# Scores of both chunks of a pair as one TensorE group, two last output transfers on ScalarE's queue, and a new order of all steps, in a gated linear attention followed by an MLP

## The chip, the cores and the metric

The kernel runs on one core of a Trainium2 chip. The metric is the time of one execution in device microseconds (us). Five engines run side by side, each in its own program order: TensorE (PE, with weight loads shown apart as PEld), VectorE (DVE), ScalarE (ACT), GpSimd (POOL) and SyncE (SP), which here only issues transfers. They meet through semaphores.

## The reference

Inputs q, k, v and a gate logit, each 4 batches x 8 heads x 768 tokens x 48 dimensions in float32; weights w_in 384x2048 and w_out 2048x384.

```python
f = 1 / (1 + exp(-f_logit))
for t in range(768):
    state = f[:, :, t, :, None] * state + k[:, :, t] (outer) v[:, :, t]
    y[:, :, t] = q[:, :, t] @ state
x = y as 3072 tokens x 384            # all heads side by side
h = x @ w_in
out = max(0.01 * h, h) @ w_out        # 3072 x 384, float32
```

## The kernel before, in words

The sequence is cut into chunks of 128 tokens. Two neighbouring chunks of one batch form a pair of 256 tokens; there are twelve pairs, and pair m belongs to batch m % 4. Pairs 0 to 3 are the starts of the four sequences. Every step works on a pair, with w = 0 or 1 for its chunk. A step is a small function with buffer numbers as arguments, and the kernel's last part, from line 451 on, is a list of 766 calls written out one under the other: each engine runs its own share of that list in that order. Nothing is scheduled at run time; an engine waits only for the semaphores of the data and buffers that its next step needs.

The steps of one pair, in the order in which they depend on each other:

- `load('K' | 'Q' | 'V' | 'F', m, s)` (line 255): SP issues the 384 KB of one input of pair m into one of three slots s. A slot is written again only when its readers are done.
- `gate_exp`, `gate_ln` (ACT, lines 259 and 262), `gate_sum` (265), `gate_pe` (TensorE, 268 and 270, a sum over earlier tokens by a triangular matrix), `gate_base` (DVE, 275), `gate_next` (279), then `decay_end`, `decay_em` and `decay_a` (ACT, 282, 285, 288): the products of gates, as exponentials of sums of logarithms.
- `scale` (294): K and Q times their decays, into one of three buffers KH.
- `turn_pe` with `turn_out` (310, 313), or `turn_dma` (305, a transposing transfer on SP's queue): KH turned into KT.
- `score(w, t, bk0, bk1)` (324): eight matmuls of 64 rows x 128 columns with 128 moving columns. Two heads lie above one another, so that the even heads use the lower 64 rows of the array and write one PSUM bank, and the odd heads use the upper 64 rows and write another.
- `mask` (DVE, 333): a bank of scores times a triangular mask, into WM.
- `mix` (TensorE, 342 and 345): WM times the values (`v_cast`, `v_spread` at 302 prepare them), plus Q times the state that the chunk begins with.
- `state_pe` (TensorE, 354, also on 64 rows), `state_dve` (361), `state_pool` (364), `put_state` (POOL, 236): the new state.
- `y_out`, then `x_pe` with `x_out` (381) or `x_dma` (387): the pair's y, turned, in XT.
- `up(g, bk, t)` (392), eight per pair: six matmuls of 256 columns into a PSUM bank; `up_act` (ACT, 408) applies the leaky ReLU.
- `down(w, h, n, bk, t)` (420): the sum over the 2048 inner dimensions, in n parts, four matmuls of 384 columns per part where n is 4, eight where n is 2. `put` copies the bank to SBUF, and `out_pair` (436) sends it. The very last chunk is made in two halves of 192 columns: `down_cols` (425), `put_cols`, `out_cols` (447).

PSUM has eight banks, and a step names the one it uses. `move` (127 on ACT, 129 on DVE and POOL) is the copy behind most steps that empty a bank, and its first argument chooses the engine. The first two pairs go by steps of their own, whose names begin with `f_`. The weights come in by POOL's queue: `load_w_in` twice (246), `load_w_out` four times (249), after `touch` has seen the gate input of pair 1 land. `idle_pe(n, bk)` (133) issues n matmuls on a buffer of zeros.

Of the kernel before, what the change touches and what calls it, by code (L numbers as in the profile page):

```python
# [15 lines left out]
def kernel(  # L16
# [10 lines left out]
    nc = tc.nc  # L27
# [429 lines left out]
    f_cast(V, 0, 1, 0, 1)  # L457
    f_ln(0, 1, 0)
    load('F', 1, 1)
    f_cast(A, 0, 0, 0, 1)  # L460
    f_gate(None, 0, (0, 0 + 1))
    f_cast(G, 0, 0, 1, 2)
# [3 lines left out]
    f_cast(G, 0, 1, 1, 2)  # L466
    idle_pe(2, 7)
    f_cast(V, 1, 0, 0, 1)
    f_turn(0, None, 2, 3)
    f_decay2(0, 'a', 0)  # L470
    f_cast(G, 1, 1, 0, 1)
    f_mul2(0, 0, 2, 0)
    idle_pe(2, 7)
    load('V', 1, 1)
    f_turn(1, None, 1, 4)
    v_cast(G, 0, 0)
    f_back(1, 0, 5)
    f_mul2(0, 1, 4, 0)
    load('Q', 1, 1)
    f_back(0, 0, 2)  # L480
    f_back_out(A, 1, 5)
    v_turn(0, 6, 6 + 1)
    touch('F', 1)
    f_back_out(A, 0, 2)
    load_w_in(0)
    load('K', 2, 2)
    score(1, 0, 0, 0 + 1)
    v_out2(A, 6, 0)
    score(0, 0, 4, 4 + 1)
    load_w_in(1)  # L490
    mask_two(0, 0)
    f_exp(1)
    load('V', 2, 2)
    load_w_out(0)
    f_state_pe(0, 0, 2)
    f_state_pe(1, 0, 6)
    idle_pe(7, 7)
    f_state_dve(0, 2)
    load_w_out(1)
    f_ln(1, 0, 0)  # L500
    load_w_out(2)
    mask_two(4, 2)
    f_ln(1, 1, 0)
    gate_exp(2)
    put_state(0, 0)
    f_gate(None, 0, (0, 0 + 1))
    load('F', 3, 0)
    load_w_out(3)
    state_dve(0, 6)
    f_decay2(1, 'e', 0)  # L510
    mix(0, 0, None, [2, 2 + 1], 0, 7)
    mix(1, 0, (0, 0), [0, 0 + 1], 0, 2)
    v_cast(G, 1, 1)
    y_out(V, 0, 7, 0)
    y_out(A, 1, 2, 0)
    f_mul2(1, 0, 3, 1)
    f_state_pool(0)
    f_decay2(1, 'a', 0)
    v_turn(1, 4, 4 + 1)
    f_cast(G, 1, 1, 1, 2)  # L520
    x_pe(0, 6)
    v_out2(V, 4, 1)
    f_cast(G, 1, 0, 1, 2)
    f_back(1, 1, 7)
    x_out(A, 6, 0)
    f_back(0, 1, 2)
    put_state(0, 1)
    f_turn(1, None, 2, 3)
    f_back_out(A, 3, 7)
    f_back_out(V, 2, 2)  # L530
    f_mul2(1, 1, 3, 1)
    f_state_pe(2, 1, 0)
    gate_ln(2)
    f_state_pe(3, 1, 1)
    up(0, 6, 0)
    gate_sum(G, 2, 0)
    up(1, 7, 0)
    f_state_dve(1, 0)
    up_act(0, 6, 0)
# [12 lines left out]
    mask_two(2, 6)
    f_state_pool(1)
    up(4, 5, 0)
    put_state(1, 1)
    up(5, 6, 0)
    up_act(4, 5, 0)
    gate_base(2, 4)
    mix(0, 1, None, [6, 6 + 1], 1, 0)
    up(6, 1, 0)  # L560
    decay_end(4, 0)
    gate_next(V, 2)
    y_out(A, 0, 0, 1)
    y_out(V, 1, 7, 1)
    up(7, 2, 0)
    decay_a(2, 0)
    down(1, 0, 4, 3, 0)
    up_act(6, 1, 0)
    x_pe(1, 7)
    up_act(7, 2, 0)  # L570
    down(0, 0, 4, 5, 0)
    x_out(V, 7, 1)
    decay_em(2, 0)
    load('F', 4, 1)
    down(0, 1, 4, 5, 0)
    up_act(5, 6, 0)
    up(0, 4, 1)
    up(1, 2, 1)
    up_act(0, 4, 1)
    up(2, 0, 1)  # L580
    up_act(1, 2, 1)
    down(0, 2, 4, 5, 0)
    up_act(2, 0, 1)
    scale(V, 0, 2, 0, 1)
    down(1, 0, 4, 4, 1)
    load('Q', 2, 2)
    down(0, 0, 4, 2, 1)
    v_cast(G, 2, 2)
    down(0, 3, 4, 5, 0)
    load('F', 5, 2)  # L590
    turn_pe(0, 1, 1)
    put(A, 0, 5, 0)
    v_spread(2, 2)
    state_pe(1, 2, 0, 7)
    gate_exp(0)
    down(1, 1, 4, 3, 0)
    load('K', 3, 0)
    gate_ln(0)
    down(1, 2, 4, 3, 0)
    state_first(2, 0, 0)  # L600
    down(1, 3, 4, 3, 0)
    load('Q', 3, 0)
    gate_exp(1)
    gate_sum(G, 0, 1)
    turn_out(V, 0, 1, 2)
    up(3, 6, 1)
    gate_ln(1)
    put(V, 1, 3, 0)
    put_state(2, 0)
    load('Q', 4, 1)  # L610
    up(4, 5, 1)
    up_act(3, 6, 1)
    scale(V, 1, 2, 0, 1)
    gate_pe(1, 3)
    up(5, 0, 1)
    up_act(4, 5, 1)
    out_pair(nc.sync, 0, 1, 0)
    down(0, 1, 4, 2, 1)
    gate_sum(G, 1, 0)
    state_dve(2, 7)  # L620
    gate_exp(2)
    load('V', 3, 0)
    turn_pe(1, 1, 1)
    gate_base(0, 3)
    up_act(5, 0, 1)
    load('V', 4, 1)
    up(6, 5, 1)
    state_pool(2, 1, 0)
    turn_out(V, 1, 1, 2)
    decay_end(3, 1)  # L630
    down(0, 2, 4, 2, 1)
    gate_ln(2)
    put_state(2, 1)
    load('V', 5, 2)
    gate_next(V, 0)
    score(1, 2, 3, 6)
    up_act(6, 5, 1)
    score(0, 2, 7, 0)
    gate_sum(G, 2, 1)
    mask(6, 8)  # L640
    up(7, 1, 1)
    decay_em(0, 1)
    down(1, 1, 4, 4, 1)
    mask(7, 9)
    up_act(7, 1, 1)
    scale(G, 0, 0, 1, 0)
    out_pair(nc.sync, 0, 0, 0)
    down(1, 2, 4, 4, 1)
    mask(0, 10)
    decay_a(0, 1)  # L650
    load('Q', 5, 2)
    down(0, 3, 4, 2, 1)
    mask(3, 11)
    load('F', 6, 0)
    mix(0, 2, None, [9, 10], 2, 5)
    put(A, 0, 2, 1)
    mix(1, 2, (2, 0), [11, 8], 2, 6)
    y_out(V, 0, 5, 2)
    scale(G, 1, 0, 1, 0)
    turn_pe(0, 0, 7)  # L660
    y_out(A, 1, 6, 2)
    down(1, 3, 4, 4, 1)
    load('K', 4, 1)
    turn_out(A, 0, 7, 0)
    x_pe(2, 5)
    gate_pe(1, 1)
    x_out(V, 5, 2)
    gate_pe(0, 0)
    put(A, 1, 4, 1)
    v_cast(G, 1, 0)  # L670
    turn_pe(1, 0, 3)
    gate_base(1, 0)
    load('Q', 6, 0)
    up(0, 2, 2)
    turn_out(A, 1, 3, 0)
    v_cast(G, 0, 1)
    gate_base(2, 1)
    up(1, 6, 2)
    v_spread(0, 0)
    load('V', 6, 1)  # L680
    decay_end(1, 2)
    decay_end(0, 3)
    state_pe(0, 1, 7, 3)
    up_act(0, 2, 2)
    score(0, 0, 5, 4)
    score(1, 0, 1, 0)
    up_act(1, 6, 2)
    up(2, 2, 2)
    load('V', 7, 0)
    gate_next(G, 1)  # L690
    mask(4, 2)
    gate_exp(0)
    up(3, 6, 2)
    state_first(3, 7, 1)
    up_act(2, 2, 2)
    down(1, 0, 4, 4, 2)
    load('K', 5, 2)
    v_cast(G, 2, 2)
    mask(1, 3)
    gate_ln(0)  # L700
    down(0, 0, 4, 7, 2)
    put_state(3, 0)
    mask(0, 0)
    load('V', 8, 2)
    up(4, 2, 2)
    up_act(3, 6, 2)
    gate_sum(V, 0, 1)
    up(5, 1, 2)
    decay_em(1, 0)
    v_spread(1, 1)  # L710
    load('K', 6, 0)
    down(0, 1, 4, 7, 2)
    up_act(5, 1, 2)
    up(6, 6, 2)
    up_act(4, 2, 2)
    out_pair(nc.sync, 1, 0, 1)
    gate_pe(1, 0)
    decay_a(1, 0)
    scale(G, 0, 1, 0, 2)
    mask(5, 1)  # L720
    mix(1, 0, (3, 0), [3, 0], 1, 1)
    out_pair(nc.sync, 1, 1, 1)
    down(0, 2, 4, 7, 2)
    gate_base(0, 0)
    up_act(6, 6, 2)
    load('F', 7, 1)
    mix(0, 0, None, [1, 2], 1, 2)
    up(7, 5, 2)
    decay_end(0, 4)
    y_out(A, 0, 2, 0)  # L730
    v_spread(2, 2)
    down(1, 1, 4, 4, 2)
    load('K', 7, 1)
    y_out(A, 1, 1, 0)
    up_act(7, 5, 2)
    down(1, 2, 4, 4, 2)
    x_pe(0, 6)
    gate_next(G, 0)
    state_dve(3, 3)
    down(1, 3, 4, 4, 2)  # L740
    x_out(A, 6, 3)
    down(0, 3, 4, 7, 2)
    gate_next(V, 2)
    decay_em(0, 1)
    up(0, 5, 3)
    scale(G, 1, 1, 0, 2)
    put(V, 0, 7, 2)
    decay_em(2, 0)
    up(1, 0, 3)
    put(V, 1, 4, 2)  # L750
    turn_pe(0, 2, 1)
    out_pair(nc.sync, 2, 1, 2)
    decay_a(2, 1)
    state_pe(2, 0, 4, 2)
    out_pair(nc.sync, 2, 0, 2)
    turn_out(V, 0, 1, 1)
    scale(G, 0, 0, 1, 1)
    decay_a(0, 0)
    up(2, 3, 3)
    load('F', 8, 2)  # L760
    state_dve(0, 4)
    turn_pe(1, 2, 1)
    load('Q', 7, 1)
    up_act(0, 5, 4)
    up(3, 6, 3)
    load('F', 9, 0)
    turn_out(V, 1, 1, 1)
    up_act(2, 3, 4)
    up(4, 7, 3)
    scale(G, 1, 0, 0, 1)  # L770
    up_act(3, 6, 4)
    score(1, 1, 3, 1)
    up_act(4, 7, 4)
    load('K', 8, 0)
    score(0, 1, 4, 5)
    mask(1, 4)
    up(5, 6, 3)
    up_act(1, 0, 4)
    mask(5, 5)
    up(6, 7, 3)  # L780
    gate_exp(2)
    state_pool(0, 0, 3)
    turn_dma(0, 1, 2)
    mask(4, 6)
    down(1, 0, 2, 1, 4)
    v_cast(G, 2, 1)
    up_act(5, 6, 4)
    mask(3, 7)
    up_act(6, 7, 4)
    put_state(0, 0)  # L790
    turn_dma(1, 1, 2)
    mix(0, 1, (0, 1), [6, 5], 0, 0)
    gate_ln(2)
    v_spread(1, 1)
    up(7, 3, 3)
    load('Q', 8, 0)
    gate_exp(0)
    down(0, 0, 2, 5, 4)
    up_act(7, 3, 4)
    v_cast(G, 1, 0)  # L800
    y_out(V, 0, 0, 1)
    mix(1, 1, (0, 0), [7, 4], 0, 4)
    load('V', 9, 2)
    gate_ln(0)
# [440 lines left out]
```

## Time and profile before

| what | value |
|---|---|
| median of the three runs (lowest, highest) | 179.95 us (179.74, 181.64) |
| the profiled execution's own time | 179.52 us |
| its span on the core | 177.8 us |
| granted TensorE clock, mean | 0.988 |
| TensorE busy | 169.2 us (95%) |
| ScalarE, VectorE, GpSimd busy | 112.9, 107.7, 73.3 us |
| HBM read, written | 25.17, 4.72 MB |

The profiled execution took 179.52 us, of which the span, from the first to the last instruction on the core, is 177.8; the 1.7 us between lie around it. In the profile, a line of a view names an engine, the line of the kernel, and what it writes and reads ("ps" is PSUM). The chain of waits goes back from the last instruction, at each step to what released it; a number behind an x counts instructions. In tables by stretch of time, busy times are given for each engine, with the granted clock of TensorE as a share of full speed.

### The profile page before, as it was taken

How to read it: one execution, taken by the hardware profiler on the slowest of the kernel's cores; microseconds unless marked ns; L12 is line 12 of the kernel's file. 1: busy time of each engine (PE TensorE's matmuls, PEld its weight loads, DVE VectorE, ACT ScalarE, POOL GpSimd, SP SyncE). 2: the span in 40 equal slices, each digit the busy share in tenths (PEclk: the TensorE clock that was granted, in tenths of full speed). 3: DMA queues.
4: the chain of work that ended last, by engine and by line, in shares of the span. 5: the costliest groups of instructions: out<-in, count | busy, mean ns of one | idle time of the engine just before them, and what ended most of it. 6: DMA issues, size and time to landing. Idle time of an engine off the chain costs nothing.

```text
span 177.8 us, 4579 instructions
## 1 busy us (share of the span) xinstructions
PE 169.2 (95%) x1843; PEld 135.0 (76%) x1843; DVE 107.7 (61%) x214; ACT 112.9 (63%) x194; POOL 73.3 (41%) x121
## 2 busy tenths in 40 slices
PE   6977999999999999999999999999999999999991
PEld 4555888677878787688697887787787796877980
DVE  5289693298599969699879592586792830100120
ACT  2978657589779696967284998396273163555700
POOL 7489420177945784595846670204055000000000
PEclk9998799999999999999999999999999999999999
DMA  5999999999999979999899998623993050120302
GB/s 133 322 324 198 210 215 213 300 274 276 322 292 278 317 201 307 131 327 226 143 236 170 298 216 174 105 46 63 116 198 88 0 135 1 32 56 4 88 20 69
DMA packets 73764, 31.68 MB, mean 178 GB/s; under 512 B 69264, under 2 KB 72464, under 8 KB 73744
## 3 DMA queue, kind: packets, MB, share of 16 engines
q1 hardware_dynamic: 71840, 28.06, 67.9%
q0 software_dynamic: 1376, 3.15, 9.3%
q8 instruction: 14, 0.23, 0.5%
q10 hardware_dynamic: 528, 0.20, 0.4%
q14 instruction: 6, 0.05, 0.1%
HBM read 25.17 MB, written 4.72 MB: 168 GB/s over the span
## 4 chain that ended last, share of the span: by engine, by line
PE 68%; DMA 16%; DVE 4%; SPq 3%; POOL 3%; ACT 2%; issue 1%; ACTq 0%
PE ps L392 29%; PE ps L420 28%; DMA w_in<-in_moe_w_in_dram 7%; DMA rawF<-in_f_logit_dram 6%; DMA kT<-kh 3%; PE ps L324 3%; DVE vb L302 3%; SPq L255 2%; PE ps L345 2%; PE ps L342 2%; PE ps L354 2%; PE ps L425 1%; ACT aa L288 1%; POOL vq L129 1%; POOL kh L294 1%
## 5 line engine op out<-in xcount | busy, mean ns | idle before, releaser
L408 ACT ACTIVATE gT<-ps 128x512 bf16<-128x512 f32 x96 | 56.4, 597 | 28.7 <-PE ps L392 24.1
L392 PE MATMUL ps<-xT,w_in 128*128 128x256 bf16 x576 | 70.6, 273 | 0.5 <-DMA w_in<-in_moe_w_in_dram 0.5
L420 PE MATMUL ps<-w_out,gT 128*128 128x384 bf16 x368 | 65.4, 326 | 0.0
L392 PEld LDWEIGHTS <-w_in 128*128 128x128 bf16 x576 | 61.0, 114 | 3.4 <-DMA w_in<-in_moe_w_in_dram 0.8
L420 PEld LDWEIGHTS <-gT 128*128 128x128 bf16 x368 | 35.3, 98 | 20.0
L333 DVE TENSOR_TENSOR wm<-ps,mask 128x512 bf16<-128x512 f32 x40 | 25.8, 685 | 15.6 <-PE ps L324 14.7
L129 DVE COPY osb<-ps 128x384 f32<-128x384 f32 (+1 forms) x13 | 6.8, 539 | 27.0 <-PE ps L420 26.0
L302 DVE COPY vb<-vq 64x384 bf16<-64x384 bf16 x40 | 18.1, 453 | 5.0 <-POOL vq L129 4.4
L294 POOL TENSOR_TENSOR kh<-rawK,em 128x384 bf16<-128x384 f32 x12 | 11.2, 952 | 13.0 <-ACT em L285 12.5
L236 POOL CAST sb<-sf 64x192 bf16<-64x192 f32 x40 | 14.8, 370 | 3.6 <-DVE sf L231 1.7
L127 ACT COPY osb<-ps 128x384 f32<-128x384 f32 (+1 forms) x12 | 5.5, 468 | 15.8 <-PE ps L420 11.2
L265 POOL TENSOR_TENSOR ls<-rawF 128x384 bf16<-128x384 f32 x9 | 9.2, 1021 | 13.6 <-ACT rawF L262 11.6
L129 POOL CAST vq<-rawV 128x768 bf16<-128x768 f32 x11 | 9.0, 826 | 11.6 <-DMA rawV<-in_v_dram 9.2
L364 POOL TENSOR_TENSOR sf<-sf,aend 128x192 f32<-128x192 f32 x14 | 8.0, 577 | 13.0 <-DVE sf L361 12.8
L361 DVE TENSOR_TENSOR sf<-sf,ps 64x192 f32<-64x192 f32 x32 | 11.2, 349 | 0.7
L259 ACT ACTIVATE rawF<-rawF 128x768 f32<-128x768 f32 x10 | 8.4, 842 | 3.3 <-DMA rawF<-in_f_logit_dram 3.2
L127 ACT CAST xn<-ps 128x384 bf16<-128x384 f32 x14 | 6.5, 481 | 5.7 <-PE ps L345 5.6
L345 PE MATMUL ps<-vb,wm 128*128 128x48 bf16 x192 | 8.7, 183 | 0.4 <-DVE wm L337 0.4
L324 PE MATMUL ps<-kT 64*128 64x128 bf16 x192 | 8.4, 217 | 0.4 <-DMA kT<-kh 0.2
L285 ACT ACTIVATE em<-rawF 128x768 bf16<-128x768 f32 x10 | 8.4, 844 | 0.4 <-DVE rawF L279 0.4
L262 ACT ACTIVATE rawF<-rawF 128x768 f32<-128x768 f32 x10 | 8.5, 848 | 0.2
L288 ACT ACTIVATE aa<-rawF 128x768 bf16<-128x768 f32 x10 | 8.3, 842 | 0.0
(83 smaller groups left out, 176.3 us busy)
## 6 DMA issues: line engine op xcount, KB each, us to landing
rawK<-in_k_dram SPq DMA_DIRECT2D x12, 384.0 KB, 5.1
rawQ<-in_q_dram SPq DMA_DIRECT2D x12, 384.0 KB, 5.3
rawV<-in_v_dram SPq DMA_DIRECT2D x12, 384.0 KB, 4.9
rawF<-in_f_logit_dram SPq DMA_DIRECT2D x11, 384.0 KB, 5.3
out_dram<-osb SPq DMA_DIRECT2D x22, 192.0 KB, 2.9
w_in<-in_moe_w_in_dram POOLq DMA_DIRECT2D x2, 768.0 KB, 10.9
w_out<-in_moe_w_out_dram POOLq DMA_DIRECT2D x4, 384.0 KB, 16.2
kT<-kh SPq DMA_TRANSPOSE x14, 4.4
```

The costliest lines, as they stand in the source:

```text
L127: eng.copy(out=out, in_=in_)
L129: eng.tensor_copy(out=out, in_=in_)
L236: G.tensor_copy(out=SB[r, b, s, :, e * D:(e + 1) * D], in_=SF[r, b])
L294: eng.tensor_mul(o[:, :, j, :, 0:D], x[:, :, j], y[:, :, j])
L302: V.tensor_copy(out=VB[64 * j:64 * j + 64, vb, w, :], in_=VQ[64 * w:64 * w + 64, t, j * KD:(j + 1) * KD])
L324: nc.tensor.matmul(bank(bks[e])[:, p * 128:(p + 1) * 128], turned(t, w, 0, p)[r], turned(t, w, 1, p)[r], start=True, stop=True)
L333: V.tensor_mul(WM[:, wm, c].rearrange("p (i n) -> p i n", n=128), bank(bk)[:, c].rearrange("p (i n) -> p i n", n=128), masks(4 if hh is No ...
L345: nc.tensor.matmul(bank(bk)[:, h * D:(h + 1) * D], WM[:, wms[h % 2], 128 * (h // 2):128 * (h // 2) + 128], VB[:, vb, w, h * D:(h + 1) * D] ...
L361: V.tensor_add(SF[r, b], SF[r, b], pt[r, :, e * D:(e + 1) * D])
L392: nc.tensor.matmul(bank(bk)[:, i * 256:(i + 1) * 256].rearrange("p (w n) -> p w n", w=2), WQ[g // 2][:, f, :, g % 2 * 2 + i], XT[:, t, :, ...
L408: A.activation(GT[:, t, 2 * g:2 * g + 2, :].rearrange("p f n -> p (f n)"), bank(bk), AF.Prelu, alpha=0.01)
L420: nc.tensor.matmul(bank(bk)[:, 0:KD], GT[:, t, ff, 128 * w:128 * w + 128], WO[:, ff, :], start=(ff == 0), stop=(ff == NF - 1))
```

## The change

The functions stay as they are; `score_pair` (329), which calls `score` for both chunks, was there before and not called. The list of calls is written in a new order and has 757 entries:

- Of the 24 calls of `score`, 20 become 10 calls of `score_pair`, each into four named banks. The four of the first two pairs stay as they were in kind.
- The first inputs are issued in another order: K, Q of pair 0 and then Q of pair 1, where K of both pairs came first; K of pair 1 is the seventh load. Farther on, V of pair 2 goes ahead of its K, and its Q goes ahead of the gates of pair 4.
- Some steps change engine. `put` runs 18 times on ACT and 5 on DVE (11 and 12 before), `y_out` 17 and 7 (14 and 10), `x_out` 5 and 2 (4 and 3), `turn_out` 3 and 3 (2 and 4); `f_back_out` once on ACT and three times on DVE (3 and 1); `v_cast` nine times on POOL and three on DVE (11 and 1); `gate_next` six on POOL, four on DVE (4 and 6); `gate_sum` eight and two (9 and 1).
- `idle_pe` issues 36 matmuls in five places, 31 in four before.
- The last chunk's four column halves: two of the four `out_cols` are issued by ACT, and both `put_cols` run on ACT.
- `load_w_out(3)` is issued later in POOL's order, behind seven other steps.

The diff, cut to these places (every call of the list moves):

```diff
     load('K', 0, 0)
-    load('K', 1, 1)
+    load('Q', 0, 0)
     idle_pe(20, 7)
-    load('Q', 0, 0)
+    load('Q', 1, 1)
     f_exp(0)
     load('V', 0, 0)
...
     load('F', 1, 1)
...
     load('F', 2, 2)
...
+    idle_pe(9, 7)
...
+    load('K', 1, 1)
...
+    load('V', 1, 1)
...
+    touch('F', 1)
+    load_w_in(0)
+    f_back_out(V, 0, 5)
+    score(0, 0, 0, 0 + 1)
+    load('V', 2, 2)
+    f_back_out(V, 1, 4)
+    score(1, 0, 2, 2 + 1)
...
+    load_w_in(1)
+    v_out2(V, 6, 0)
...
+    load('K', 2, 2)
+    load_w_out(0)
...
+    load('F', 3, 0)
...
+    score(0, 1, 0, 0 + 1)
+    v_out2(A, 2, 1)
+    gate_base(2, 5)
+    score(1, 1, 6, 6 + 1)
+    put_state(0, 1)
+    up(0, 4, 0)
...
+    up(4, 5, 0)
...
+    load('Q', 2, 2)
...
+    load('F', 4, 1)
...
+    scale(V, 0, 2, 0, 1)
...
+    state_pe(1, 2, 2, 3)
+    scale(V, 1, 2, 0, 1)
+    turn_pe(0, 1, 5)
...
+    down(0, 3, 4, 1, 0)
...
+    turn_pe(1, 1, 4)
...
+    score_pair(2, (7, 2), (5, 4))
...
-    score(1, 2, 3, 6)
-    up_act(6, 5, 1)
-    score(0, 2, 7, 0)
...
-    score(1, 1, 3, 1)
...
-    score(0, 1, 4, 5)
...
-    put_cols(V, 1, 0, 6, 2)
-    out_cols(nc.sync, 23, 1, 0, 2)
-    out_cols(nc.sync, 23, 0, 0, 2)
-    put_cols(A, 1, 192, 7, 2)
-    out_cols(nc.sync, 23, 0, 192, 2)
-    out_cols(nc.sync, 23, 1, 192, 2)
+    put_cols(A, 1, 0, 6, 3)
+    out_cols(A, 23, 1, 0, 3)
+    out_cols(nc.sync, 23, 0, 0, 3)
+    put_cols(A, 1, 192, 7, 3)
+    out_cols(A, 23, 0, 192, 3)
+    out_cols(nc.sync, 23, 1, 192, 3)
```

More of the change, by code (lines that the diff above doesn't have):

```diff
@@ L481 @@
[L481 to L503, printed above, removed]
+    f_back(0, 0, 5)
@@ new lines @@
+    up(7, 6, 1)
+    mask(4, 11)
+    y_out(A, 0, 2, 2)
+    down(1, 0, 4, 7, 1)
+    load('V', 5, 2)
+    gate_sum(V, 1, 1)
+    decay_em(0, 1)
+    down(1, 1, 4, 7, 1)
+    put(A, 0, 1, 0)
+    load('K', 4, 1)
+    scale(V, 0, 0, 1, 2)
+    gate_pe(0, 2)
+    mix(1, 2, (2, 0), [10, 11], 2, 5)
+    put(A, 1, 0, 0)
+    gate_pe(1, 4)
+    down(1, 2, 4, 7, 1)
+    y_out(A, 1, 5, 2)
+    scale(G, 1, 0, 1, 2)
+    gate_base(1, 4)
+    load('K', 5, 2)
+    up_act(7, 6, 1)
+    turn_pe(0, 2, 5)
+    gate_base(2, 2)
@@ new lines @@
+    x_pe(2, 1)
+    decay_end(4, 2)
+    decay_end(2, 3)
+    down(0, 3, 4, 3, 1)
+    load('K', 6, 0)
+    x_out(A, 1, 2)
+    down(1, 3, 4, 7, 1)
+    gate_next(V, 1)
+    put(A, 0, 3, 1)
+    turn_pe(1, 2, 6)
+    v_cast(G, 0, 0)
+    turn_out(V, 0, 5, 0)
+    out_pair(nc.sync, 0, 1, 0)
+    decay_a(1, 0)
+    up(0, 0, 2)
+    out_pair(nc.sync, 0, 0, 0)
+    turn_out(V, 1, 6, 0)
+    v_cast(G, 1, 1)
+    put(A, 1, 7, 1)
+    up(1, 1, 2)
+    load('Q', 6, 0)
+    up_act(0, 0, 2)
+    out_pair(nc.sync, 1, 0, 1)
@@ new lines @@
+    down(0, 0, 4, 1, 2)
+    scale(V, 0, 1, 0, 0)
+    load('V', 6, 0)
+    up_act(6, 6, 2)
+    mix(0, 0, None, [0, 3], 0, 3)
+    down(0, 1, 4, 1, 2)
+    decay_em(2, 1)
+    scale(G, 1, 1, 0, 0)
+    state_dve(3, 7)
+    turn_pe(0, 0, 5)
+    y_out(A, 0, 3, 0)
+    mask(2, 1)
+    state_pe(0, 1, 4, 6)
+    load('K', 7, 1)
+    turn_out(A, 0, 5, 1)
+    down(1, 0, 4, 7, 2)
+    mix(1, 0, (3, 0), [1, 2], 0, 3)
+    v_spread(2, 1)
+    up_act(5, 0, 2)
+    load('F', 8, 2)
+    turn_pe(1, 0, 2)
@@ new lines @@
+    y_out(A, 1, 3, 0)
+    up(7, 5, 2)
+    turn_out(A, 1, 2, 1)
+    down(0, 2, 4, 1, 2)
+    load('Q', 7, 1)
+    state_pool(3, 1, 1)
+    state_dve(0, 4)
+    x_pe(0, 0)
+    scale(G, 0, 2, 1, 1)
+    up_act(7, 5, 2)
+    down(1, 1, 4, 7, 2)
+    load('V', 7, 1)
+    x_out(A, 0, 3)
+    down(1, 2, 4, 7, 2)
+    gate_exp(1)
+    score_pair(1, (0, 3), (2, 4))
+    load('V', 8, 2)
+    v_cast(V, 0, 0)
+    up(0, 5, 3)
+    gate_exp(0)
+    state_pool(0, 0, 2)
+    mask(0, 4)
+    down(1, 3, 4, 7, 2)
@@ L580 @@
[L580 to L602, printed above, removed]
@@ L651 @@
[L651 to L672, printed above, removed]
@@ L673 @@
[L673 to L766, printed above, removed]
@@ new lines @@
+    state_pe(2, 1, 1)
+    x_out(A, 4, 1)
+    state_pe(0, 2, 7, 6)
+    gate_pe(1, 3)
+    gate_sum(G, 2, 0)
+    state_dve(0, 1)
+    load('Q', 10, 1)
+    up(0, 2, 1)
+    gate_base(0, 3)
+    up(1, 4, 1)
+    up_act(0, 2, 0)
+    v_cast(G, 2, 1)
+    put(V, 0, 5, 0)
+    up(2, 1, 1)
+    turn_dma(0, 0, 1)
+    decay_end(3, 0)
+    up_act(1, 4, 0)
+    state_dve(3, 7)
+    gate_next(G, 0)
+    up(3, 2, 1)
+    up_act(2, 1, 0)
+    turn_dma(1, 0, 1)
+    score_pair(0, (3, 7), (5, 4))
+    state_pool(3, 0, 5)
@@ new lines @@
+    y_out(A, 1, 6, 2)
+    x_dma(0, 0)
+    v_spread(2, 0)
+    score_pair(1, (4, 6), (2, 3))
+    state_pe(1, 1, 0)
+    turn_dma(0, 1, 0)
+    down(0, 0, 2, 1, 2)
+    state_pool(2, 1, 0)
+    mask(6, 5)
+    put_state(2, 1)
+    mask(4, 6)
+    turn_dma(1, 1, 0)
+    down(0, 1, 2, 1, 2)
+    mask(3, 4)
+    state_dve(2, 5)
+    x_dma(2, 1)
+    mix(0, 1, (2, 1), [6, 5], 0, 6)
+    put(A, 0, 1, 3)
+    state_dve(3, 0)
+    up(0, 3, 0)
+    state_pool(2, 0, 3)
+    put(A, 1, 7, 3)
+    y_out(V, 0, 6, 1)
```

1117 lines of the change are left out of this document (554 added, 563 removed).

## The prediction

> **What bounds the kernel now.** I read the busy shares first, then the chain of waits, then the stretches by time, then SP's queue.
>
> ```profile
> span 177.8 us, 4579 instructions
> ...
> PE 169.2 (95%) x1843; PEld 135.0 (76%) x1843; DVE 107.7 (61%) x214; ACT 112.9 (63%) x194; POOL 73.3 (41%) x121
> ```
>
> TensorE is busy for 95% of the span, so other engines matter only where they hold it up. The chain of waits says when it is TensorE that counts:
>
> ```profile
> 11.62 12.63 DMA w_in<-in_moe_w_in_dram
> 24.26 0.05 issue
> 24.30 1.50 PE ps L392 x12
> ...
> 34.18 0.45 PE ps L310 x8
> 34.62 0.45 PE ps L354 x16
> 35.07 2.06 PE ps L420 x12
> 37.13 1.31 PE ps L392 x12
> ...
> 41.12 0.65 PE ps L420 x4
> 41.77 0.55 PE ps L324 x16
> 42.32 0.78 PE ps L392 x6
> ...
> 76.57 0.33 PE ps L324 x8
> ...
> 171.21 2.65 PE ps L425 x32
> ```
>
> Until 24.30 the kernel waits for weights: the second half of w_in is issued at 11.62 and is there at 24.26, and the fifth `up` starts on it. From there to 173.86 (171.21 + 2.65) the chain is TensorE's almost throughout; then one copy and the output transfers are left. So three things can change the time: the date at which TensorE has its data, the amount of its work after that, and the tail. The reader should also see in these rows that a change of shape costs something. Twelve full-height matmuls of `up` take 1.31, six thus 0.655. Sixteen score matmuls on 64 rows take 0.55 and eight take 0.33: eight more cost 0.22, so 0.11 is paid on entering. The six matmuls behind the sixteen take 0.78, which is 0.12 more than 0.655: that is paid on leaving. A run of 64-row work therefore costs about 0.22 us beside its matmuls.
>
> **Part 1, the groups.** Counted along TensorE's order, with `score` and `state_pe` both 64-row work, the list before has 16 such runs from `up(3, 6, 1)` on, which starts at 37.13 in the row above. The new list has 14 from `turn_pe(1, 1, 4)` on. Although 20 calls become ten pairs, five of the ten pairs already stood together before, and state work that used to touch a score group now stands alone in places. So it is two runs, and 2 x 0.22 = 0.44 us. All the rest from these two points to the end is the same list of matmuls, but for four `up` before against four quarter `down` now: 4 x 0.655 = 2.62 against 4 x 0.65 (row 41.12) = 2.60. TensorE's work from point to end is 0.46 us less. A pair asks for four free banks at once, and `up` steps queue behind it on TensorE. No row of before prices that: between nothing and one mask per group. I take nothing, since its banks are mostly emptied a whole `up` or `down` earlier in the list, and keep 1 us of it for the range.
>
> **Part 2, the start.** The loads of all inputs go through SP's queue, the weights through POOL's, onto the same transfer engines.
>
> ```profile
> q0 software_dynamic: 1255, 2.86, 93.5%
> q1 hardware_dynamic: 1190, 0.45, 15.8%
> ```
>
> These are the two queues between 14 and 30 us: the weights moved 2.86 MB, the inputs 0.45, a little over one load. What isn't in by 14 us waits until the weights are through:
>
> ```profile
> L255 SPq DMA_DIRECT2D rawK<-in_k_dram x1: 1327/1327/1327, 10.4 to 10.4; - x1
> DMA to landing us min/median/max: 18.7/18.7/18.7
> ...
> L255 SPq DMA_DIRECT2D rawF<-in_f_logit_dram x1: 5287/5287/5287, 25.5 to 25.5; - x1
> DMA to landing us min/median/max: 10.5/10.5/10.5
> ```
>
> The ninth load (K of pair 2) is issued at 10.4 and lands at 29.1; the twelfth (gates of pair 4) is issued at 25.5 and lands at 36.0. The new order keeps the same eight loads in front, K and Q of both first pairs among them, so the first two pairs get their data by the same time. The gates of pair 1, on whose landing POOL issues w_in, stay fifth; POOL has two casts fewer ahead of it. I cost w_in's landing at no change: 24.3. `load_w_out(3)` moves behind seven other steps of POOL; its queue is still full with three parts ahead of it, so it costs nothing as long as it is issued before they are through. Three copies of the first pair move from ACT to DVE, ahead of its first mask. Their cover is the wait for w_in; if it is too short, the first half microsecond is swallowed at the next place, and what is beyond that shows in full.
>
> The twelfth load is now Q of pair 2, and there the new order has a wait. `turn_pe(1, 1, 4)` needs Q scaled by DVE in two instructions:
>
> ```profile
> L294 DVE TENSOR_TENSOR kh<-rawQ,aa 128x384 bf16<-128x384 f32 x12 | 8.1, 712 | 0.1
> ```
>
> 36.0 + 2 x 0.712 gives 37.4, with the hop to TensorE 37.45. By its own work TensorE would be there sooner. From 24.30 it has eleven `up` (7.2), six `x` transposes (0.34, by the row at 34.18), six quarter `down` (3.9), `state_pe` with its leaving (0.45 + 0.11) and one `turn_pe` (0.45): 12.45, and 0.2 for the slow first twelve matmuls (1.50 against 1.31), so 36.95. It waits 0.5 us. Behind it on TensorE everything queues. The good side: any lateness of up to 0.5 us before this point costs nothing. Point to end is now 37.45 + (173.86 - 37.13) - 0.46 = 173.72, a gain of 0.14. What small waits before had behind that point are kept in this sum.
>
> **Part 3, steps that change engine.** ACT takes seven `put`, three `y_out`, an `x_out` and a `turn_out` from DVE.
>
> ```profile
> L408 ACT ACTIVATE gT<-ps 128x512 bf16<-128x512 f32 x96 | 56.4, 597 | 28.7 <-PE ps L392 24.1
> ...
> L127 ACT CAST xn<-ps 128x384 bf16<-128x384 f32 x14 | 6.5, 481 | 5.7 <-PE ps L345 5.6
> ...
> L285 ACT ACTIVATE em<-rawF 128x768 bf16<-128x768 f32 x10 | 8.4, 844 | 0.4 <-DVE rawF L279 0.4
> ```
>
> Where it is tightest, from `turn_pe(1, 1, 4)` to `score_pair(1, ...)`, TensorE has nine `up` (5.9), sixteen quarter `down` (10.4), five `turn_pe` (2.25) and small groups that I estimate at 4.6, so 23.2 us. ACT has nine `up_act` (5.4), ten passes over a whole gate or decay tile (8.4) and thirteen copies of 0.48 or more (6.2): 20 us at least. That is cover of 3 us at most, and I cost the moves at nothing beneath it; without the cover each microsecond shows (rival two).
>
> **Part 4, the tail.**
>
> ```profile
> 174.34 0.55 SPq L447 DMA_DIRECT2D out_dram<-osb  x1
> 174.94 0.59 SPq L447 DMA_DIRECT2D out_dram<-osb  x1
> ```
>
> ```profile
> rawF<-in_f_logit_dram ACTq DMA_DIRECT2D x1, 192.0 KB, 3.7
> rawF<-in_f_logit_dram SPq DMA_DIRECT2D x1, 192.0 KB, 3.3
> out_dram<-osb SPq DMA_DIRECT2D x2, 96.0 KB, 2.2
> out_dram<-osb SPq DMA_DIRECT2D x4, 48.0 KB, 1.9
> ```
>
> The last two transfers wait for one copy, and SP issues them one after the other, 0.60 apart; each lands 1.9 later. From two queues both can go at 174.34, and 0.60 is saved. Of two equal halves issued together at the start, ACT's landed 0.4 later than SP's, so the gain may be 0.2. ACT's earlier issue lies before its last copy, beside 1.3 us (half of 2.65) of matmuls, and holds nothing up. I take 0.5, near the upper end, as 48 KB is a quarter of those halves. The Trainium skill ("DMA: Bandwidth & Descriptors", Rules for kernel authors) says that two transfers to disjoint partition halves serialize from two queues as well, and are not worth splitting. The trace only half agrees: the second was issued before the first had landed and still landed 0.6 behind it, its issue distance. By that rule strictly the tail would stay and the sum end 0.5 later.
>
> **The sum.** -0.14 - 0.5 = -0.64 us. Against the profiled execution, 179.52 with a span of 177.8, that is 178.9. Its 179.52 stands 0.43 under the median of 179.95, so against the median it is 179.3.
>
> **Rivals.** One: TensorE doesn't wait for Q of pair 2, because that load comes earlier or DVE has done K's part and more. For it: a single queue place decides. Against: the weights' end at about 31 us is the same. Then the point moves to 36.95 and the gain is 0.18 + 0.46 + 0.5 = 1.1: 178.8.
>
> Two, slower: ACT becomes the bound in the stretch of part 3, and TensorE waits for its banks. For it: 20 us is a lower end, as copies of larger tiles take longer than 0.48. Against: over the whole span ACT is at 63%. It decides from the point where its work and gaps together pass 23.2; with 0.15 us of extra per copy and gap on 32 steps, 4.8 us, it would be at 24.8 and cost 1.6: 180.9.
>
> Three, slower: the clock.
>
> ```profile
> 16.00:18.00 2.00, 1.79 (x19) 1.47 (x19) 1.92 (x2) 1.57 (x3) 1.94 (x6) 0.66 1.09 195
> 18.00:20.00 2.00, 1.82 (x19) 1.57 (x17) 1.32 (x2) 1.30 (x3) 0.80 (x2) 0.50 1.12 212
> ```
>
> The granted clock (third number from the end) falls to half between 18 and 20, in the sparse work before the weights are in. The new order has two score groups more before the first `up`, and the same gaps around K of pair 1. If the dip lasts 2.5 us longer, work of 1.3 us comes late; 0.5 is swallowed by the wait for Q, 0.8 stays: 180.1. The Trainium skill ("TensorE: Matmul & The Clock Gate", Part 1) ties full speed to some 3.4 us of sustained work. The trace agrees as to the half, 0.50, and as to its coming behind sparse work.
>
> Four: the tail's change does nothing, since ACT's transfer lands later by as much: 179.8. It is what the page's rule in part 4 would give.
>
> **Numbers.** Chances: forecast 0.50, rival one 0.14, two 0.16, three 0.14, four 0.06. Within 1% (1.8 us, about what a measurement of this kernel can tell from no change) lie all five at their own prices. Rival one with no small wait left behind that point could pass -1.8, and so could the forecast if w_in came earlier: 0.10 for faster. Rival two at twice its price, or two and three together, pass +1.8: 0.10 for slower. That leaves 0.80. The range reaches from 178.1, the lower side of rival one, to 181.0, rival two; 1 us for four free banks lies within it.
>
> **What would show it.** In the profile after: the chain has w_in landing at 24.3 and TensorE from there; a wait of about 0.5 on a transpose at L310 near 37 us with DVE's `kh` ahead of it; L324 in groups of sixteen of 0.55, none of eight; the last two transfers issued within 0.1 us of each other, and landing together. Wrong would be: w_in later than 25; waits of TensorE on ACT between 37 and 61 us; a TensorE share of that stretch under 98%; or a last output matmul after 174.

## The result, and the profile after

The changed kernel took 178.85 us (median of seven runs, 178.67 to 179.38). The kernel before, run beside it on the same chip, took 181.18 (179.74 to 182.01). The ratio of the two times is 0.9889, with a 95% interval from 0.9853 to 0.9924. The profiled execution took 178.72 us with a span of 177.0, against 179.52 and 177.8 before: 0.8 us less.

The two differences, 2.3 us of medians and 0.8 us of profiled executions, don't contradict each other. The kernel before scatters: its executions here lie between 179.7 and 182.0, and its profiled one is near the lower end. Those of the changed kernel lie within 0.7 us. In a second comparison the kernel before had a median of 179.56 and the changed one 178.59, ratio 0.994 (0.9918 to 0.9962). So the gain of the medians is 0.6% in one comparison and 1.1% in the other, and the larger one has in it that the kernel before scatters more. What makes it scatter is not shown by the runs below.

The page of the changed kernel has the span, the busy shares and the engines' shares of the chain of waits:

```profile
span 177.0 us, 4593 instructions
...
PE 168.6 (95%) x1848; PEld 135.3 (76%) x1848; DVE 101.1 (57%) x204; ACT 119.3 (67%) x206; POOL 73.9 (42%) x119
...
PE 84%; DMA 10%; SPq 3%; ACT 1%; POOL 1%; issue 0%
```

TensorE's share of the span is what it was. What changed is the last line: TensorE holds 84% of the chain that ended last, where the page of before gives it 68%:

```profile
PE 68%; DMA 16%; DVE 4%; SPq 3%; POOL 3%; ACT 2%; issue 1%; ACTq 0%
```

The changed kernel is bound by TensorE's own work from the landing of w_in on.

The chain of waits of the changed kernel, with the date, the duration and the work of each piece:

```profile
10.45 0.85 ACT rawF L141
...
11.36 0.19 POOL seen L242
11.55 0.87 POOL w_in L246
12.42 12.65 DMA w_in<-in_moe_w_in_dram
25.07 0.05 issue
25.12 1.50 PE ps L392 x12
...
37.10 0.65 PE ps L420 x4
37.75 0.45 PE ps L310 x8
...
170.90 2.65 PE ps L425 x32
173.55 0.02 issue
173.57 0.32 ACT osb L127
```

The second half of w_in lands at 25.07, not at 24.26, and the fifth `up` begins 0.82 later than before (25.12 against 24.30). The landing is the last thing that this `up` waits for, but most of the lateness is TensorE's own. Early on it waits 2.3 us, until 15.4, for a copy by GpSimd that stands behind the issues of the weights (first line below, from the view of waits; in the kernel before TensorE has no such wait). Its last matmuls ahead of the fifth `up` begin at 24.68 (second line). The other two lines are from `puts_on_dve`, an experiment below, in which w_in had landed at 24.84 and didn't hold TensorE up: there the `up` follows the same matmuls by 0.21.

```profile
PE ps L176 <- POOL kh L129: 2.3, 1, 2.3
...
24.68 0.36 PE L345 MATMUL ps<-vb,wm 128*128 128x48 bf16 x8
...
25.01 0.36 PE L345 MATMUL ps<-vb,wm 128*128 128x48 bf16 x8
25.22 1.53 PE L392 MATMUL ps<-xT,w_in 128*128 128x256 bf16 x12
```

So I estimate from these rows that with w_in in time the `up` would have begun at about 24.9. About 0.6 of the 0.82 is TensorE's own lateness, and about 0.2 the landing.

The transpose at L310, `turn_pe(1, 1, 4)`, begins at 37.75 and nothing releases it but the matmuls ahead of it. The last output matmul ends at 173.55. From the fifth `up` to that end TensorE needs 148.43 us, against 173.86 - 24.30 = 149.56 before: 1.13 less.

The view of waits, asked for TensorE from 24 us to the end, has these lines in the kernel before (time in all, number, longest). In this profile of the changed kernel it has none (a second one has 0.3 on w_in):

```profile
PE ps L392 <- DMA w_in<-in_moe_w_in_dram: 0.3, 1, 0.3
PE ps L324 <- DMA kT<-kh: 0.2, 1, 0.2
```

The tail of the changed kernel, from the timeline by engine (a row with x2 holds two instructions), and the landing times of these transfers from the view of line 447:

```profile
172.80 1.58 SPq L447 DMA_DIRECT2D out_dram<-osb  x2
173.57 0.32 ACT L127 COPY osb<-ps 128x192 f32<-128x192 f32 x1 [0.96 <-PE ps L425]
173.92 0.50 ACTq L447 DMA_DIRECT2D out_dram<-osb  x1
```

```profile
L447 ACTq DMA_DIRECT2D out_dram<-osb x2: 497/527/557, 172.6 to 173.9; - x2
L447 SPq DMA_DIRECT2D out_dram<-osb x2: 467/508/548, 172.8 to 173.9; - x2
...
DMA to landing us min/median/max: 1.8/2.0/2.1
```

Both last halves are issued at 173.92. SP's lands at 175.76 and ACT's at 176.05. From the last output matmul to the last landing are now 2.50 us, against 176.92 - 173.86 = 3.06 before: 0.56 less.

The account of the profiled pair: 0.82 later at the start, 1.13 less from there to the end of TensorE's work, 0.56 less in the tail. That is -0.87, against a measured -0.8 of span.

### The profile page after: what moved, and what is told of

It is laid out like the page before. It is cut to its first block, busy times and chain, and to the rows that moved or that the text cites. A ratio compares the mean times of both kernels' runs of the same rounds, so it can differ in the third digit from the quotient of the medians.

```text
span 177.0 us, 4593 instructions
## 1 busy us (share of the span) xinstructions
PE 168.6 (95%) x1848; PEld 135.3 (76%) x1848; DVE 101.1 (57%) x204; ACT 119.3 (67%) x206; POOL 73.9 (42%) x119
## 4 chain that ended last, share of the span: by engine, by line
PE 84%; DMA 10%; SPq 3%; ACT 1%; POOL 1%; issue 0%
PE ps L392 35%; PE ps L420 34%; DMA w_in<-in_moe_w_in_dram 7%; PE ps L324 3%; DMA rawF<-in_f_logit_dram 3%; SPq L255 2%; PE ps L354 2%; PE ps L345 2%; PE ps L342 2%; PE ps L310 2%; PE ps L425 1%; PE ps L381 1%; PE ps L268 1%; POOL w_in L246 0%; ACT rawF L141 0%; PE ps L270 0%
## 5 line engine op out<-in xcount | busy, mean ns | idle before, releaser
L392 PE MATMUL ps<-xT,w_in 128*128 128x256 bf16 x576 | 68.2, 273 | 0.1
L408 ACT ACTIVATE gT<-ps 128x512 bf16<-128x512 f32 x96 | 56.3, 597 | 17.5 <-PE ps L392 14.0
L420 PEld LDWEIGHTS <-gT 128*128 128x128 bf16 x368 | 34.5, 98 | 19.8
L127 ACT COPY osb<-ps 128x384 f32<-128x384 f32 (+1 forms) x20 | 8.9, 467 | 18.6 <-PE ps L420 14.2
L129 DVE COPY osb<-ps 128x384 f32<-128x384 f32 x5 | 2.8, 556 | 29.2 <-PE ps L420 15.8
L302 DVE COPY vb<-vq 64x384 bf16<-64x384 bf16 x40 | 14.3, 357 | 2.5 <-PE ps L345 1.9
L294 POOL TENSOR_TENSOR kh<-rawQ,aa 128x384 bf16<-128x384 f32 x12 | 12.9, 1092 | 1.6 <-issue 1.5
L129 POOL CAST vq<-rawV 128x768 bf16<-128x768 f32 x9 | 7.7, 859 | 12.7 <-PE ps L354 6.1
L127 ACT CAST xn<-ps 128x384 bf16<-128x384 f32 x17 | 7.8, 481 | 4.5 <-PE ps L345 4.2
L294 DVE TENSOR_TENSOR kh<-rawK,em 128x384 bf16<-128x384 f32 x12 | 9.4, 823 | 2.0 <-DMA rawK<-in_k_dram 1.8
L279 POOL TENSOR_TENSOR rawF<-rawF 128x384 f32<-128x384 f32 x6 | 6.0, 998 | 7.1 <-DVE rawF L275 7.0
```

What stands on the lines that cost most here:

```text
L127: eng.copy(out=out, in_=in_)
L129: eng.tensor_copy(out=out, in_=in_)
L294: eng.tensor_mul(o[:, :, j, :, 0:D], x[:, :, j], y[:, :, j])
L302: V.tensor_copy(out=VB[64 * j:64 * j + 64, vb, w, :], in_=VQ[64 * w:64 * w + 64, t, j * KD:(j + 1) * KD])
L392: nc.tensor.matmul(bank(bk)[:, i * 256:(i + 1) * 256].rearrange("p (w n) -> p w n", w=2), WQ[g // 2][:, f, :, g % 2 * 2 + i], XT[:, t, :, ...
L408: A.activation(GT[:, t, 2 * g:2 * g + 2, :].rearrange("p f n -> p (f n)"), bank(bk), AF.Prelu, alpha=0.01)
```

## The experiments

Each kernel was timed in turns with the kernel before on the same chip, and each ratio is to that kernel's time, with its 95% interval. The kernel before had medians from 179.56 to 181.18 in these comparisons, so medians from different comparisons can't be set against one another to a few tenths. The theories to tell apart at the outset: the gain comes from longer runs of one shape on TensorE and from the two queues at the end (mine), or from the new order of the loads.

**The kernel before, once more.** No edit.

> The kernel before, unchanged, against itself. Theory one: its executions scatter by 2 us (179.74 to 182.01 so far) because of something in its own schedule, such as transfers that land just in time; then a slow execution shows waits of TensorE on transfers or on DVE after 24.3 us that the recorded one (span 177.8) doesn't have, and the changed kernel beside it stays within 0.7 us. Theory two: the chip scatters; then the changed kernel's variants in this call scatter as much.

Measured: 180.47 (179.07 to 181.91), ratio 1.0032 (0.9996 to 1.0068). In its profiled execution the second half of w_in landed at 23.58, 0.7 earlier than in the first trace, and the span was 177.7, the same to 0.1. The lead of 0.53 at 27 us had shrunk to 0.11 behind the wait for a transposed K at 73.7. Most of an earlier start is lost in the kernel before. As this execution was one of the shorter ones (179.44), it doesn't show what lengthens the others. The chip alone doesn't do it: two variants of the changed kernel, timed beside it, had spreads of 0.6 us (all four last transfers on SP's queue) and 3.1 (the weights ahead of ScalarE's exponential).

**All four last transfers on SP's queue.** In the changed kernel:

```diff
-    out_cols(A, 23, 1, 0, 3)
+    out_cols(nc.sync, 23, 1, 0, 3)
...
-    out_cols(A, 23, 0, 192, 3)
+    out_cols(nc.sync, 23, 0, 192, 3)
```

> The changed kernel with all four last column halves issued by SP, as before. Theory: the last transfer is issued 0.6 later and lands at 176.5 to 176.6 in place of 176.05, 0.5 us slower. Rival: the two transfers serialize however they are issued, no difference.

Measured: 179.08 (178.96 to 179.53), ratio 0.9957 (0.994 to 0.9974). The view of line 447 now has one queue:

```profile
L447 SPq DMA_DIRECT2D out_dram<-osb x4: 546/570/588, 172.9 to 174.8; - x4
...
DMA to landing us min/median/max: 1.9/2.0/2.0
```

The last issue is at 174.8 instead of 173.9, and the time from the last output matmul to the last landing is 3.13 us, 0.63 more. The medians stand 0.49 above the second comparison's 178.59 and 0.23 above the first one's 178.85. By the traces the second queue is worth 0.63 us, and by medians of different comparisons 0.2 to 0.5. A gain over the kernel before remains without it.

**The pairs taken apart.** In the changed kernel each of the ten `score_pair` became two `score`, the second one further down the list, behind an `up` or `down`. One of ten:

```diff
-    score_pair(0, (3, 7), (5, 4))
+    score(0, 0, 3, 7)
     up(4, 1, 1)
+    score(1, 0, 5, 4)
```

In this kernel one mask reads its bank before that chunk's scores are written, so its output isn't the reference's; all the work is done.

> The changed kernel with each score pair taken apart again: the second chunk's scores stand behind the next full-height step of TensorE. Ten more runs of 64-row work. Theory: 10 x 0.22 = 2.2 us slower, 181.0, all of it between 38 and 173 us. Rival: entering costs and leaving is hidden by weight loads: 1.1 us slower. Second rival: the groups cost nothing by themselves and the gain came from the order: no difference.

Measured: 181.76 (181.2 to 182.47), ratio 1.0108 (1.008 to 1.0136), span 180.0. From the fifth `up` to its last output matmul TensorE took 151.32 us, where a second profile of the changed kernel has 148.42: 2.90 more for ten runs more. The chain around 92 us in that second profile of the changed kernel, and then in the kernel with the pairs apart:

```profile
92.10 0.55 PE ps L324 x16
92.65 2.75 PE ps L392 x24
```

```profile
93.08 0.33 PE ps L324 x8
93.41 0.78 PE ps L392 x6
94.19 0.33 PE ps L324 x8
```

One score group of sixteen matmuls, 0.55, has become two of eight, 0.33 each, which is 0.11 more, and the six `up` matmuls between them pay the leaving: 0.78 instead of 0.655. That is 0.11 + 0.12 for each run, as in the trace of before, and 2.3 for ten; TensorE's timeline behind the transpose at 37.8 us has 24 runs of 64-row work here and 14 in the changed kernel. Of the rest, 0.6, I followed one piece: at 56.3 us a transpose at L310 stood 0.23 longer than in the changed kernel, since VectorE got its scores later.

**The pairs taken apart, with that mask moved behind its scores.**

> The ten score pairs taken apart as in split_pairs, with one mask moved behind the scores that it reads. Theory: ten more runs of 64-row work at 0.22 us: 2.2 us slower than after_again. Rival: half of it, as leaving is hidden: 1.1.

Measured: 182.64 (182.09 to 184.58), ratio 1.0174 (1.0126 to 1.0223), span 181.9. I expected 2.2 us over the changed kernel; it is 4.05 by the medians, 4.6 by the spans. From the fifth `up` to the end it is 152.22, 3.80 over the changed kernel's second profile, and w_in landed 0.8 later than there, at 26.13, although the edit lies far behind it. The waits of TensorE from 24 us on:

```profile
PE ps L392 <- DVE wm L333: 0.9, 1, 0.9
PE ps L392 <- DMA w_in<-in_moe_w_in_dram: 0.7, 1, 0.7
```

The moved mask explains 0.9: an `up` at 119 us waits for the bank that this mask empties. What remains of the 3.80 are the 2.9 of the first version. Taking the pairs apart thus costs 0.22 per run on TensorE, and beyond that whatever now comes too late behind it.

**The weights ahead of ScalarE's exponential.** Comparing the traces I saw why the weights are issued later: in the new list `f_exp(1)`, which overwrites the gates of pair 1, stands ahead of `touch('F', 1)`. GpSimd's look at these gates must then wait for ScalarE (0.85 from 10.45 in the chain above). I held this, by way of w_in's later landing, for the cause of the 0.82 at the start.

```diff
+    touch('F', 1)
     f_exp(1)
-    touch('F', 1)
```

> The changed kernel with the copy that waits for the gates of pair 1 (L242) ahead of ACT's exponential of them, not behind it. Theory: w_in is issued 0.8 us earlier, lands at 24.3 in place of 25.07, and TensorE's fifth up starts then; at turn_pe(1, 1, 4) it meets Q of pair 2 (landed 35.62 + 1.42 + 0.05 = 37.1 where TensorE alone would be at 36.95), so 0.65 us of it is kept: 178.2 against 178.85. Rival: w_in isn't what TensorE waits for, or the wait for Q takes all of it: 178.8.

Measured: 179.38 (178.02 to 181.09), ratio 0.9949 (0.992 to 0.9978), with a scatter like that of the kernel before. The changed kernel wasn't timed in the same comparison. The kernel with all four last transfers on SP's queue was, and took 179.08 although it lacks the second queue.

> The kernel of touch_first once more, for a second profiled execution. There the weights were issued as early as in the kernel before (11.54 against 11.62), but their second half took 13.42 us to land instead of 12.6 and came at 24.96. If that was this one execution: issued at 11.5, landed at 24.1 to 24.3, the fifth `up` 0.8 us earlier than in the changed kernel. If the transfer itself is longer in this order of loads, so that an earlier issue brings nothing: landed at 24.9 to 25.1 again. The time: median 179.4 again, spread over 2 us, V of pair 2 landing near 29.8.

Measured: 179.49 (178.51 to 179.92), ratio 0.9936 (0.9907 to 0.9965). The landing times of w_in's two halves (least, median, most) are in the view of line 246; here of touch_first_again and then of the changed kernel:

```profile
L246 POOL DMA_DIRECT2D w_in<-in_moe_w_in_dram x2: 786/864/941, 10.7 to 11.6; - x2
...
DMA to landing us min/median/max: 10.0/11.8/13.6
```

```profile
L246 POOL DMA_DIRECT2D w_in<-in_moe_w_in_dram x2: 786/864/941, 11.5 to 12.4; - x2
...
DMA to landing us min/median/max: 9.1/10.9/12.7
```

Issued 0.8 earlier, the second half took 0.9 longer and landed at 25.20. In touch_first it had been the same: issued at 11.54, landed at 24.96. So my cause fell as to the landing: the wait for the exponential does delay the issue, but in these two profiles an earlier issue didn't bring an earlier landing. TensorE itself did get earlier: its wait for GpSimd's copy is 1.1 us instead of 2.3, and it then waits 0.8 for w_in. What else the earlier issue brings shows in the V loads issued at 9.3 and 10.4, again for touch_first_again and then for the changed kernel:

```profile
L255 SPq DMA_DIRECT2D rawV<-in_v_dram x2: 1111/1276/1441, 9.3 to 10.4; - x2
...
DMA to landing us min/median/max: 5.1/12.6/20.1
```

```profile
L255 SPq DMA_DIRECT2D rawV<-in_v_dram x2: 1111/1219/1327, 9.2 to 10.4; - x2
...
DMA to landing us min/median/max: 4.9/5.5/6.0
```

The ninth load, V of pair 2, lands at 30.6 when the weights come 0.3 us behind it, and at 16.4 when they come 1.1 behind it. All later loads then shift: the gates of pair 5 land at 41.05 instead of 38.16, and the chain of touch_first_again runs through them:

```profile
34.55 6.51 DMA rawF<-in_f_logit_dram
...
41.08 0.84 ACT rawF L259
...
45.46 1.27 DVE kh L294
...
46.78 0.56 PE ps L310 x7
```

Against the changed kernel its TensorE is 0.12 behind at the fifth `up`, 0.69 behind at this transpose and 1.18 behind at 57 us.

**The weights a little later than that.** The same edit, with the look at the gates made four times.

```diff
+    touch('F', 1)
+    touch('F', 1)
+    touch('F', 1)
+    touch('F', 1)
     f_exp(1)
-    touch('F', 1)
```

> The changed kernel with GpSimd's look at the gates of pair 1 ahead of ScalarE's exponential, as in touch_first, but made four times, so that the weights are issued about 0.4 us later than there (11.0 instead of 10.60; 11.48 in the changed kernel). If what costs touch_first its median and its scatter is that the weights overtake the ninth load (V of pair 2, issued at 10.36): here V gets through by about 16.5 instead of 29.8, and the time is that of the changed kernel or a little less, 178.2 to 178.6, with a scatter under 1 us. If the scatter comes from the early weights as such, or V is still overtaken, the median stays near 179.4 and the spread near 3 us.

Measured: 178.91, ratio 0.994 (0.9907 to 0.9973). Ten of the twelve executions lie between 178.37 and 179.70; the other two took 182.06. The weights were issued at 11.32, later than I meant (11.0) and only 0.16 ahead of the changed kernel's. The span of the profiled execution is 177.0, that of the changed kernel. V of pair 2 was through at 16.28, and w_in landed at 24.94. TensorE does its early steps up to 1.4 us sooner and then waits for w_in all the same.

The median is about 0.5 below those of touch_first and touch_first_again, as the theory of the ninth load asks. But the three ratios (0.9949, 0.9936, 0.994) can't be told apart, and the spread of the ten, 1.3 us, is not under 1 and not below the 1.4 of touch_first_again. So the traces show what the ninth load does to the later loads. That the level or the scatter of the times comes from it is not shown.

**The weights still later.** In the changed kernel the look goes at K of pair 1, and in the kernel before at the gates of pair 2; they land 2.5 and 1.3 us after the gates of pair 1.

```diff
-    touch('F', 1)
+    touch('K', 1)
```

> The changed kernel, with the copy ahead of the weights waiting for K of pair 1 (the seventh load, 12.9): w_in is issued 1.4 us later than in the changed kernel. Theory: in the changed kernel TensorE waits for w_in and for nothing after it, so the whole of it shows: 1.2 to 1.4 slower, 180.1, as tight. Rival: a later load sets the time; then it is no slower, as these come earlier still.

Measured: 180.46 (179.59 to 180.85), ratio 1.0034 (1.0011 to 1.0057), 1.9 over the changed kernel where I expected 1.2 to 1.4 through w_in. The chain shows another way:

```profile
12.78 0.18 POOL seen L242
12.97 0.92 POOL w_in L246 x2
...
14.62 1.65 POOL w_out L249 x3
16.28 0.52 POOL kh L129
...
16.84 1.04 PE ps L176 x8
```

GpSimd waits for its look at 12.78, and behind it are queued five weight transfers and then the copy `kh` of the second pair. That copy is 1.5 us later than in the changed kernel, and TensorE's wait for it grows from 2.3 to 3.8. The weights, landed at 26.60, come in time for a TensorE that is late already: its fifth `up` begins at 26.84.

The clock has a part in this too. In this profile the granted clock is 0.50 from 15.7 to 22.5 us, 6.8 us in all; in the profile of the changed kernel it is 0.50 from 16.6 to 20.0, 3.4 us. And the twelve executions fall into two groups: nine with a mean granted clock of 0.981 took 180.42 to 180.85, three with 0.987 or 0.988 took 179.59 to 179.70. So about 0.9 of the 1.9 goes with the longer dip of the clock, and about 1.0 is left for the later copy. None of the sixteen executions of the changed kernel had a mean under 0.986. Whether the longer wait for the copy brings the longer dip on, no run shows.

```diff
-    touch('F', 1)
+    touch('F', 2)
```

> The kernel before, with the copy ahead of the weights waiting for the gates of pair 2 (the sixth load) and not of pair 1 (the fifth): w_in is issued 1.2 us later. Theory: the ninth load lands at 16.5 in place of 29, all later ones 1 us or more earlier; w_in lands at 25.4; the scatter of 2 us and more shrinks to under 0.8, and the median stays or falls (179.2 to 179.6) although the weights come later. Rival: the scatter comes from the transposes by transfer between 66 and 150 us, which the new order asks for earlier; then it stays, and the time grows by 1.1.

Measured: 181.4 (181.07 to 182.32), ratio 1.0101 (1.0066 to 1.0136). I expected the kernel before to gain or to stay, as its ninth load would get through. It did get through (16.2), but w_in landed at 25.06, 0.8 later, and a further 0.8 was lost between the fifth `up` and the end. The two longest of its waits from 24 us on:

```profile
PE ps L324 <- DMA kT<-kh: 0.5, 1, 0.5
PE ps L345 <- DVE vb L302: 0.3, 1, 0.3
```

The order of before doesn't use the early ninth load. The spread was 1.3 us, against 1.6 of the unedited kernel beside it, where I expected under 0.8, and the level was higher.

**The changed kernel once more**, beside the two kernels with later weights and the second one with the pairs apart. No edit.

> The changed kernel, unchanged, beside the others of this call. Theory (the ninth load gets through ahead of the weights, so later loads come 1 us or more earlier and leave room): 178.7 to 179.4 in every execution, while the kernel before scatters from 179.0 upward. Rival (the scatter is the chip's): it scatters as much here.

Measured: 178.59 (178.39 to 178.98), ratio 0.994 (0.9918 to 0.9962), span 177.3, w_in landed at 25.35.

**Four copies back on VectorE.** In the changed kernel, the first four `put`:

```diff
-    put(A, 0, 1, 0)
+    put(V, 0, 1, 0)
...
-    put(A, 1, 0, 0)
+    put(V, 1, 0, 0)
...
-    put(A, 0, 3, 1)
+    put(V, 0, 3, 1)
...
-    put(A, 1, 7, 1)
+    put(V, 1, 7, 1)
```

> The changed kernel with four of its copies of output blocks (the first four `put`, between 43 and 49 us) moved from ScalarE back to VectorE. In the changed kernel VectorE is busy 19.08 of 20 us from 40 to 60, ScalarE 17.44. If the moves of steps between engines bring and cost nothing, as I predicted: 178.6, within 0.3. If they are what keeps VectorE from being the bound there: four copies of about 0.55 are 2.2 us more on VectorE, 21.3 for 20 us, and TensorE waits up to 1.3 us for it: 179.3 to 179.9.

Measured: 178.78 (178.53 to 179.52), ratio 0.9936 (0.9908 to 0.9964), span 177.1. The busy times by stretch of the changed kernel (TensorE, its weight loads, VectorE, ScalarE, GpSimd, the granted clock, the DMA share, GB/s), and then of this one:

```profile
40.00:60.00 20.00, 20.00 (x258) 15.91 (x253) 19.08 (x33) 17.44 (x32) 13.77 (x18) 1.00 1.07 297
```

```profile
40.00:60.00 20.00, 20.00 (x261) 15.98 (x256) 19.68 (x37) 16.06 (x28) 13.99 (x17) 1.00 1.09 298
```

VectorE is busy 19.68 of 20 us, and TensorE still doesn't wait. These four moves, of the twelve copies that ACT took over, neither bring nor cost anything. My reckoning of 21.3 us for VectorE was too high. The four copies are in the stretch with 2.2 us, but others took less there than in the changed kernel: the eight at L302 416 ns each instead of 483, the one at L279 543 instead of 1006. Why they did is not shown; in the changed kernel's second profile those at L302 took 416 too.

## Why the prediction was right, and where not

**The bound.** Right. From the landing of w_in on, TensorE sets the time, and more so than before.

**Part 1, the groups.** The mechanism is right and its price too: 0.11 on entering and 0.12 on leaving stand in the rows of the pairs taken apart. The count is right as well: TensorE's timelines have 16 runs of 64-row work behind this point before, and 14 now. The gain from point to end was mis-sized. From `up(3, 6, 1)` before, at 37.13, to the end were 136.73 us; from `turn_pe(1, 1, 4)` now, at 37.75, they are 135.80. That is 0.93 less, where I had 0.46. I kept "what small waits before had behind that point" in the sum, and they went: 0.2 of them is the wait for a transposed K in the list of waits. The other 0.27 is in no line of the views, and stays open. No wait for four free banks showed; the microsecond that I kept for it wasn't needed.

**Part 2, the start.** Here a step failed: "I cost w_in's landing at no change: 24.3". It landed at 25.07, in a second profile at 25.35, and "later than 25" was one of my own signs of being wrong. I had counted GpSimd's casts ahead of the weights but hadn't seen that ScalarE's exponential now stands ahead of GpSimd's look at the same buffer. That explains the issue, 0.8 later. It doesn't explain the landing: with the issue put back, it was 24.96 and 25.20. What lengthens the transfer in the new order is not settled.

A second term was missing: when TensorE itself is ready for the fifth `up`. I wrote that the first two pairs get their data by the same time. The data were there, K of pair 1 at 12.88, but GpSimd's copy of it stands behind the look and the issues of the weights, and TensorE waited for this copy until 15.4. With w_in at 24.3 it would still have begun at about 24.9, by the estimate above.

The reckoning behind it held. I had TensorE at the transpose at 36.95 by its own work; with 0.82 added, that is 37.77, and it was 37.75. The wait of 0.5 for Q of pair 2 wasn't there, since TensorE came later and Q earlier: issued at 15.2 as the view of SP's loads has it, it landed 20.4 us later, at 35.6 instead of 36.0. As I wrote, lateness up to 0.5 at the start costs nothing there. Of the 0.82, 0.30 showed at that point (37.75 against the 37.45 forecast). The ninth load, which by my working waits until the weights are through, got through ahead of them.

**Part 3, steps that change engine.** Right: nothing. ScalarE is busy 17.44 of 20 us between 40 and 60, and TensorE 20.00. Rival two, ScalarE as the bound, fell.

**Part 4, the tail.** Right: 0.56 where I took 0.5, and 0.63 by taking it away. The last two transfers are issued together and land 0.29 apart, the second by ACT's queue, nearly as the halves at the start did (0.4). So the sign that I had named, landing together, came only nearly true. With all four on one queue the last issue is 0.9 later, and the landing, counted from the last output matmul, 0.63 later. Rival four fell with it. The Trainium skill ("DMA: Bandwidth & Descriptors", Rules for kernel authors) says that two transfers to disjoint partition halves serialize even from two queues, and advises one transfer over all partitions instead. These runs agree only in part: the second half lands 0.29 behind the first, and two queues were still worth 0.63 against one. The single transfer that the page advises was not tried.

**Rival one**, no wait for Q, held as to its condition, but its gain went into the later start. **Rival three**, a longer dip of the clock, fell for the changed kernel: in both profiles the clock is at 0.50 for 3.4 us, and on average it is 0.990, 0.988 before. Elsewhere it shows: with the weights still later the dip was 6.8 us long, and 0.9 us of time went with it. A dip of 6.8 us in the profile of puts_on_dve, from 14.4 to 21.2, cost nothing that the times show: its fifth `up` began at 25.22, and the execution took 178.83.

**The sum.** Predicted for the profiled execution: 178.9; it took 178.72. Three sizes were off, +0.30 at the point, -0.47 behind it and -0.06 in the tail, and they cancel in part. That the total is so close is in part luck, and says less than the parts do. Against the median I had 179.3 for 178.85. But the forecast change was 0.64 us, and the medians taken side by side differ by 2.3 us, and by 1.0 in the second comparison. I gave 0.80 to a change within 1%, and the comparisons have 1.1 and 0.6%, on both sides of that line. I measured from a median of three runs of a kernel that scatters by 2 us, and said nothing of the scatter. That the changed kernel scatters so much less is an effect I didn't foresee.

## What to carry to other kernels

When several transfers share the engines, look at which one is the last to be issued ahead of a long burst: 0.8 us decided here whether a load was there at 16 or at 30 us, and the loads behind it followed. When a step moves ahead of another that reads the same buffer in place, look for who waits on the other engine, and what is queued behind that wait. And a run of another shape on TensorE has a price of its own, here 0.22 us, to be counted in runs, not in matmuls.

## What the runs showed of the hardware that I had not expected

The weights' queue and the loads' queue share evenly in packets, not in bytes. Between 17 and 30 us, while both have work, the changed kernel's two queues moved (packets, MB, share of the engines' time):

```profile
q0 software_dynamic: 1021, 2.34, 93.5%
q1 hardware_dynamic: 1018, 0.39, 16.7%
```

The counts are equal, and were so in the kernel before (1006 and 1004) and in touch_first_again (998 and 998). A packet of the weights holds 2.3 KB, one of the loads 0.38, so the loads get about a seventh of the bytes. A load issued 0.3 us ahead of the first weights takes 20.1 us, one issued 1.1 us ahead 6.0 (9.3 in the second kernel with the pairs apart).

Issued earlier, at 11.61 instead of 12.42, the second half of w_in took longer by as much (13.6 instead of 12.7 us). This was so in both profiles with the early issue in the new order. But the length also varies by itself: in the second kernel with the pairs apart it was 13.44 with the issue at 12.70. In the kernel before an issue at 11.62 took 12.63. I have no explanation that a run shows.
